# Attention block with a peer mixture: which chunks of the output projection use plain products, and which engine prepares wo's combinations

## The chip, the cores and the metric

The kernel runs on one core of a Trainium2 chip. The metric is device time in microseconds for one launch. Before the change the median of three runs is 1894.39 us (1894.09 to 1894.46).

## The reference

Two branches see the same x (2048 tokens, 1024 features). Branch a is multi-head attention with 32 heads of 32 features, followed by an output projection with wo (1024 x 1024). Branch b picks one expert of 64 per token and head. A gate mixes them.

```python
g = sigmoid((x * gate_w).sum(-1))
qkv = x @ wqkv;  q, k, v = 32 heads of 32
p = softmax(q @ k.T * 32**-0.5)
a = (p @ v).reshape(2048, 1024) @ wo
b = sum over heads of gelu(x . u[e]) * v[e]      # e: the best expert by two small keys
out = g * a + (1 - g) * b
```

## The kernel before

All products run in pairs of rounded numbers: a number is split into a high part (rounded to the type fp32r) and a low part (the rest), and a product of two numbers becomes three matmuls, high by high, high by low, low by high. `split(hi, lo, src)` (L91) does this with a copy on ScalarE (L92) and a subtraction on VectorE (L93).

**Stages.** First queries and keys (L328), then the router of branch b (L404), then the values x @ wv in two halves of 512 columns (L569), then attention by heads (scores L773, exponentials on ScalarE L783, weighted values L794), then the output projection, which the profile calls the tail here.

**Value stage.** `values(ts, half)` makes tiles of 128 tokens, 24 matmuls each; `values_out` (L572) copies each from PSUM to SBUF on ScalarE and stores it by ScalarE's own DMA queue. The last tile goes to a PSUM tile named "o" that belongs to the pool of the next stage, and VectorE copies it out (L575). Between the tiles 4 to 13 of the second half stand `load_early` and `split_early` in turns (L691): they load blocks of wo, form four combinations of them (VectorE, L669), split each (ScalarE copy to a tile "th" of which there are two, VectorE subtraction in place) and store both parts to DRAM tensors t0 to t3, each with h and l for the parts. There are four such rounds of four blocks and a fifth one for the expert table v (tensors vph, vpl). These combinations are those of a Strassen-like scheme.

**Tail.** The 2048 tokens are projected in eight chunks of 256 (`W`). A chunk of the attention output (OC, read from od) is first scaled by one over the row sums times the gate (RB, read from rd).

- Chunk 0 uses plain products: `wo_mm` (L980), 12 matmuls for each of the 8 blocks `kc` of 128 features, 96 in all, on four PSUM banks. Their operands OH and OL, and wo's parts woh and wol, are split as they go (`split_hi`, `split_lo`, L1003 to L1015). The block kc = 7 needs the row sums of the last four heads.
- Chunks 1 to 7 use the scheme with seven products instead of eight: `unit(n)` (L1133) makes 7 `product`s (L1063, 12 matmuls each, L1070) with operands A11, S3, S1, S2, A12, S4, A22 that `operand` (L1048) splits, and with blocks of wo (B11, B21, B22) or the stored combinations (T1 to T4, loaded by `load_t`, L1025). Branch b is added by `av_mm` (L987), 8 matmuls a chunk, so a unit has 92 matmuls and a plain chunk 104.
- While a unit runs, `ahead` prepares the operands of the next chunk. For chunk 1 there is no unit before it: its first product A11 B11 is placed before block kc = 7 of chunk 0, its operands are made between, and the scaling of chunk 2 begins only after the first products of `unit(1)` (L1205).

**The row sums' way.** `finish(H - 1)` and `norm_sums` store the last head's output and sums (od, smd); `load_r` reads the sums of the last group back (rr), `norm_r` takes reciprocals and stores them (rd), and `load_chunk` reads them in a broadcast (rb for chunk 0, the tile accd for others). All of these are DMAs on SyncE's queue (SP), and in order there; only the blocks 0 to 6 of chunk 1 are loaded by GpSimd's queue (L1081). In the same SP queue stand the loads of the combinations: T3 = t2 ahead of the store to smd (L1084), T1 = t0 between the read of rr and the store to rd (L1097), T2 = t1 after (L1104), T4 = t3 after chunk 2 (L1123). Each is 2 MB in its two parts.

**Places.** PSUM has eight banks, named pa0 to pa7 in the tail and used in turn. `post` is the space of rb0, reused for results before their stores. z0, z1 and the two "acc" tiles are reused for operands.

Of the kernel before, what the change touches and what calls it, by code (L numbers as in the profile page):

```python
# [9 lines left out]
F32 = mybir.dt.float32  # L10
F32R = mybir.dt.float32r
# [5 lines left out]
S = 2048  # L17
# [6 lines left out]
W = 256  # L24
# [6 lines left out]
def gated_mha_peer_kernel(ctx, tc, xT, wqkv, wv, wo, wq, k12, ug, v, out):  # L31
# [59 lines left out]
    def split(hi, lo, src, on=None):  # L91
        nc.scalar.activation(hi, src, AF.Copy)  # L92
        (on or nc.vector).tensor_tensor(out=lo, in0=src, in1=hi.bitcast(F32), op=OP.subtract)  # L93
# [8 lines left out]
    def bank():  # L102
        i = bank_no[0] % 8
        bank_no[0] += 1
        return ps1.tile([128, 512], F32, name=f"bk{i}")
# [455 lines left out]
    def values(ts, half, bank=bank):  # L561
        ps = [bank() for _ in ts]
        for kc in range(KC):
            wh, wl = WV[half, kc]
            for t, p in zip(ts, ps):
                tok = slice(t * 128, (t + 1) * 128)
                for a, b, first, last in ((xh, wh, kc == 0, False), (xh, wl, False, False),
                                          (xl, wh, False, kc == KC - 1)):
                    nc.tensor.matmul(p, a[:, kc, tok], b, start=first, stop=last)  # L569
        return ts, ps, half  # L570

    def values_out(ts, ps, half, copy=lambda o, p: nc.scalar.activation(o, p, AF.Copy)):  # L572
        for t, p in zip(ts, ps):
            o = vw.tile([128, 512], F32, name="vo")
            copy(o, p)  # L575
            dma(VD[half][t * 128:(t + 1) * 128, :], o, nc.scalar)
# [70 lines left out]
    load_kq(0, Z)  # L647
    load_shift(0, Z)
    values_out(*fin0)
    values_out(*values(list(range(4)), 1))  # L650

# [11 lines left out]
                    dma(raw[j][64 * k:64 * k + 64, :], v[:, j * 512:(j + 1) * 512])  # L665

    def split_early(i):
        def sub(out, a, b):
            nc.vector.tensor_tensor(out=out, in0=a, in1=b, op=OP.subtract)  # L669

        def parts(t, dst_hi, dst_lo):
            hi, lo = th.tile([128, 512], F32R, name="th"), t.bitcast(F32R)
            split(hi, lo, t)
            dma(dst_hi, hi)
            dma(dst_lo, lo)

        if i < KC // 2:
            b11, b12, b21, b22 = (raw[j] for j in range(4))
            sub(b11, b12, b11)
            sub(b12, b22, b12)  # L680
            sub(b22, b22, b11)
            sub(b21, b21, b22)
            for k, t in enumerate((b11, b22, b12, b21)):
                parts(t, *(d[:, i, :] for d in TD[k]))
        else:
            for j in range(2):
                parts(raw[j], *(d[:, j * 512:(j + 1) * 512] for d in VPD))

    for t in range(4, NT - 1):
        values_out(*values([t], 1))  # L690
        (load_early, split_early)[t % 2](t // 2 - 2) if t < NT - 2 else None  # L691

    ps1.close()
    pso = Pool("pso", space=PSUM, side="right")
# [277 lines left out]
        AT[n] = fin.tile([128, W], F32R, name="at", bufs=3)  # L972
        dma(AT[n], ATD[:, n * W:(n + 1) * W])

    def wo_mm(pa, kcs, first, last):
        for kc in kcs:
            wh, wl = (W0[0][:, 0], W0[0][:, 1]) if kc == 0 else (woh[kc], wol[kc])
            for a, b, i in ((OH[0], wh, 0), (OH[0], wl, 1), (OL[0], wh, 2)):
                for tt, half in pa:
                    nc.tensor.matmul(pa[tt, half], a[:, kc, tt * 128:(tt + 1) * 128],  # L980
                                     b[:, half * 512:(half + 1) * 512],
                                     start=(first and kc == kcs[0] and i == 0),
                                     stop=(last and kc == kcs[-1] and i == 2))
# [36 lines left out]
    def places(t, *names):  # L1020
        t = t.rearrange("p (a k m) -> p a k m", k=HC, m=128)
        for i, name in enumerate(names):
            AP[name] = t[:, 2 * i], t[:, 2 * i + 1]
# [39 lines left out]
    def product(a, b, *av):  # L1063
# [8 lines left out]
                                 stop=(k == HC - 1 and i == 1))  # L1072
        return ps

    ps_odd = None
    pa = {(i, half): bank() for i in range(W // 128) for half in range(2)}
    wo_mm(pa, [0], True, False)
    finish(H - 1)
    sm = pso.tile([128, 512], F32, name="o")
    list(rowsum(sm, *(P[H - 1, NT - i] for i in (1, 2)), ACC.pop(H - 1)))  # L1080
    load_chunk(1, 0, KC - 1, nc.gpsimd)  # L1081
    for n in range(2):
        load_at(n)
    load_t(2, [zp.tile([128, S], F32R, name="z1")], [fin.tile([128, S], F32R, name="t3l")])  # L1084
    places(fin.tile([128, S], F32R, name="s31"), "S3", "S1")
    places(wk.tile([128, S], F32R, name="acc"), "A11", "A12")
    split_hi(1)
    for kc in range(1, KC - 1):
        split_hi(kc + 1)
        if kc == 1:  # L1090
            norm_sums(H - 1, sm)
            load_r(G - 1)
            pso.close()
        split_lo(kc)
        if kc == 4:

            load_t(0, *([keep.tile([128, S], F32R, name=f"wo_raw{i}")] for i in range(2)))  # L1097
        wo_mm(pa, [kc], False, False)
    norm_r(G - 1)
    for n in range(2):  # L1100
        load_chunk(n, KC - 1, KC)
    split_lo(KC - 1)
    split(woh[0], wol[0], raw_wo(0))
    load_t(1, *([keep.tile([128, S], F32R, name=f"wo_raw{i}")] for i in range(2, 4)))  # L1104
    ps_odd = Pool("ps_odd", space=PSUM)
    for (i, half), ps in pa.items():
        av_mm(0, i, half, ps)
    scale_o(1, 0)
    operand(1, "A11")
    BP.update({f"B{i + 1}{j + 1}": [[part[i * HC + k][:, j * 512:(j + 1) * 512] for k in range(HC)]  # L1110
                                    for part in (woh, wol)] for i in range(2) for j in range(2)})
    p1 = product("A11", "B11")
    o = OC[0][:, KC - 1, :]
    nc.vector.tensor_mul(o, o, RB[0][:, KC - 1, :])
    split(OH[0][:, KC - 1, :], OL[0][:, KC - 1, :], o)
    wo_mm(pa, [KC - 1], False, True)
    operand(1, "S3")
    scale_o(1, 1)
    operand(1, "S1")
    load_chunk(2, 0, KC)  # L1120
    load_at(2)

    load_t(3, *([part[k][:, 512:] for k in range(HC)] for part in (woh, wol)))  # L1123
    places(zp.tile([128, S], F32R, name="z0"), "S2")
    places(wk.tile([128, S], F32R, name="acc"), "S4", "A22")
    post = rb0.rearrange("p k m -> p (k m)").rearrange("p (a m) -> p a m", m=512)

    def osb():
        return wk.tile([128, 512], F32, name="osb")

    ORDER = ("A11", "S3", "S1", "S2", "A12", "S4", "A22")

    def unit(n, p1):  # L1133


        u2, u3, u5 = (post[:, i] for i in range(3))
        last = n == S // W - 1

        def ahead(*names):
            if last:  # L1140
                return
            for name in names:
                if name == "A11":
                    scale_o(n + 1, 0)
                    scale_o(n + 1, 1)
                operand(n + 1, name)

        c1 = osb()
        nc.scalar.activation(c1, p1, AF.Copy)
        if n == 1:  # L1150
            for (i, half), ps in pa.items():
                r = osb() if i == half == 0 else post[:, 2 * i + half]
                if half:
                    nc.scalar.activation(r, ps, AF.Copy)
                else:
                    nc.vector.tensor_copy(r, ps)
                store(0, i, half, r)
            for name in ("S2", "A12", "S4", "A22"):
                operand(n, name)
        if n + 2 < S // W:  # L1160
            load_chunk(n + 2, 0, KC)
            load_at(n + 2)
        if n > 1:
            ahead("A11")
        p7 = product("S3", "T3")
        if n > 1:
            ahead("S3")
        p5 = product("S1", "T1")
        if n > 1:
            ahead("S1")  # L1170
        p6 = product("S2", "T2")
        tt(u2, c1, p6)
        tt(u3, u2, p7)
        tt(u2, u2, p5)
        tt(u5, u3, p5)
        if n > 1:
            ahead("S2")

        def c11():
            p2 = product("A12", "B21", n, 0, 0)  # L1180
            pieces = 2 if last else 1
            for i in range(pieces):
                c = slice(i * 512 // pieces, (i + 1) * 512 // pieces)
                tt(c1[:, c], c1[:, c], p2[:, c])
                store(n, 0, 0, c1, c)

        def c12():
            p3 = product("S4", "B22", n, 0, 1)
            tt(u2, u2, p3)
            store(n, 0, 1, u2)  # L1190

        def c22():
            ps = bank()
            av_mm(n, 1, 1, ps, True, True)
            tt(u5, u5, ps)
            store(n, 1, 1, u5)

        def c21():
            p4 = product("A22", "T4", n, 1, 0)
            tt(u3, u3, p4)  # L1200
            store(n, 1, 0, u3)

        if not last:
            c11()
            ahead(*((() if n > 1 else ORDER[:4]) + ("A12",)))  # L1205
        c12()
        ahead("S4")
        c22()
        c21()
        ahead("A22")  # L1210
        if last:
            c11()

    for n in range(1, S // W):
        unit(n, p1 if n == 1 else product("A11", "B11"))
    ps_odd.close()
    ps_even.close()
    fin.close()
# [32 lines left out]
```

## Time and profile before

| what | value |
|---|---|
| median of 3 runs | 1894.39 us |
| the profiled execution, its own time | 1892.16 us |
| span of its trace | 1890.4 us |
| mean granted TensorE clock | 0.995 |
| TensorE busy | 1860.9 us (98% of the span), 10187 matmuls |
| VectorE busy | 1285.2 us (68%) |
| ScalarE busy | 1179.9 us (62%) |
| GpSimd busy | 148.8 us (8%) |

The 1.8 us between the span and the execution's time lie before and after the traced instructions. A group of the profile is named out<-in by the program's tile names; "idle before, releaser" says how long the engine stood still ahead of the instruction and what ended this. "PEclk" or "granted clock" is the share of full speed at which the throttle let TensorE run. Where matmuls follow one another without a wait, their starts are 0.227 us apart in this kernel (128x128 by 512 columns), although each one's own duration is about 0.39 us, since they are pipelined.

The stages on the trace's clock: queries and keys to 391 us, router to 481 us, values 481 to 668 us, attention 668 to 1696 us, the tail from there to the end.

### The profile page before, as it was taken

How to read it: one execution, taken by the hardware profiler on the slowest of the kernel's cores; microseconds unless marked ns; L12 is line 12 of the kernel's file. 1: busy time of each engine (PE TensorE's matmuls, PEld its weight loads, DVE VectorE, ACT ScalarE, POOL GpSimd, SP SyncE). 2: the span in 40 equal slices, each digit the busy share in tenths (PEclk: the TensorE clock that was granted, in tenths of full speed). 3: DMA queues.
4: the chain of work that ended last, by engine and by line, in shares of the span. 5: the costliest groups of instructions: out<-in, count | busy, mean ns of one | idle time of the engine just before them, and what ended most of it. 6: DMA issues, size and time to landing. Idle time of an engine off the chain costs nothing.

```text
span 1890.4 us, 25992 instructions
## 1 busy us (share of the span) xinstructions
PE 1860.9 (98%) x10187; PEld 1143.2 (60%) x10187; DVE 1285.2 (68%) x1066; ACT 1179.9 (62%) x1461; POOL 148.8 (8%) x183
## 2 busy tenths in 40 slices
PE   9999999999999899999999999999999999998899
PEld 7877777888888654444444444444444444446787
DVE  4522224867521368888888888888888888885774
ACT  4211111200222289999999999999999999992221
POOL 0000000035200000000000000000000000010000
PEclk9999999999999999999999999999999999999999
DMA  5777774420234767777778787777777777757651
GB/s 211 279 269 258 263 271 138 137 73 2 79 103 145 257 163 169 158 176 157 178 161 191 161 186 163 182 167 179 175 168 174 160 166 176 184 123 251 211 172 57
DMA packets 118468, 325.81 MB, mean 172 GB/s; under 512 B 15892, under 2 KB 50084, under 8 KB 94088
## 3 DMA queue, kind: packets, MB, share of 16 engines
q1 hardware_dynamic: 80904, 177.83, 30.8%
q0 software_dynamic: 14976, 103.29, 26.3%
q10 hardware_dynamic: 22464, 43.00, 7.1%
q8 instruction: 81, 1.33, 0.3%
q14 instruction: 43, 0.35, 0.1%
HBM read 152.36 MB, written 72.10 MB: 119 GB/s over the span
## 4 chain that ended last, share of the span: by engine, by line
PE 93%; DMA 4%; DVE 1%; ACT 1%; SPq 0%; issue 0%; ACTq 0%; DVEq 0%
PE ring L773 28%; PE o L794 25%; PE bk L328 16%; PE pa L1070 7%; PE bk L569 6%; PE bk L404 5%; PE bk L214 2%; PE bk L275 2%; PE ring L807 1%; DMA smd<-ssb 1%; DMA t1h<-th 1%; PE pa L987 1%; DMA t3l<-wvraw 1%; DMA wvraw<-in_wo 1%; PE pa L980 0%; SPq L74 0%
## 5 line engine op out<-in xcount | busy, mean ns | idle before, releaser
L783 ACT ACTIVATE P<-ring 128x512 f32<-128x512 f32 (+2 forms) x1034 | 914.8, 983 | 21.8 <-PE ring L773 8.3
L822 DVE TENSOR_TENSOR acc<-acc,P 128x2048 f32<-128x2048 f32 x319 | 731.0, 2292 | 74.6 <-ACT P L783 48.5
L794 PE MATMUL o<-P,V 128*32 128x512 f32 x3840 | 464.8, 599 | 0.0
L773 PE MATMUL ring<-z,z 98*128 98x512 f32 x1024 | 272.2, 407 | 1.4 <-ACT P L783 1.1
L773 PE MATMUL ring<-Q,K 98*128 98x512 f32 x1024 | 271.7, 407 | 0.2 <-ACT P L783 0.2
L773 PEld LDWEIGHTS ring<-z,z 98*128 98x128 f32 x1024 | 182.0, 188 | 144.8 <-ACT P L783 76.0
L773 PEld LDWEIGHTS ring<-Q,K 98*128 98x128 f32 x1024 | 182.1, 188 | 143.8 <-ACT P L783 73.8
L794 PEld LDWEIGHTS o<-P,V 128*32 128x32 f32 x3840 | 98.8, 109 | 223.1 <-issue 214.2
L92 ACT ACTIVATE hi<-bk 128x512 fp32r<-128x512 f32 x64 | 37.6, 598 | 242.7 <-PE bk L328 226.6
L328 PE MATMUL bk<-xh,whi 128*128 128x512 f32 x448 | 176.2, 393 | 0.1
L328 PE MATMUL bk<-xh,wlo 128*128 128x512 f32 x448 | 174.4, 389 | 0.0
L328 PE MATMUL bk<-xl,whi 128*128 128x512 f32 x448 | 174.4, 389 | 0.0
L93 DVE TENSOR_TENSOR lo<-bk,hi 128x512 fp32r<-128x512 f32 x64 | 44.1, 690 | 188.5 <-ACT hi L92 184.1
L816 POOL DMA_DIRECT2D accd<-P x95 | 81.6, 859 | 1108.0 <-ACT P L783 622.8
L820 DVE TENSOR_TENSOR acc<-P 128x2048 f32<-128x2048 f32 x32 | 73.4, 2292 | 74.2 <-ACT P L783 74.2
L328 PEld LDWEIGHTS bk<-xh,whi 128*128 128x128 f32 x448 | 84.1, 188 | 24.2 <-issue 6.7
L569 PE MATMUL bk<-wvh,xh 128*128 128x512 f32 x248 | 96.7, 390 | 0.0
L569 PE MATMUL bk<-wvh,xl 128*128 128x512 f32 x248 | 96.5, 389 | 0.0
L569 PE MATMUL bk<-wvl,xh 128*128 128x512 f32 x248 | 96.5, 389 | 0.0
L328 PEld LDWEIGHTS bk<-xh,wlo 128*128 128x128 f32 x448 | 84.1, 188 | 17.7
L328 PEld LDWEIGHTS bk<-xl,whi 128*128 128x128 f32 x448 | 84.2, 188 | 17.0
L1070 PE MATMUL pa<-woh,acc 128*128 128x512 f32 x224 | 74.4, 397 | 7.8 <-ACT acc L92 7.8
(189 smaller groups left out, 1703.8 us busy)
## 6 DMA issues: line engine op xcount, KB each, us to landing
accd<-P POOLq DMA_DIRECT2D x95, 1024.0 KB, 7.5
wqt<-in_wq SPq DMA_DIRECT2D x32, 1024.0 KB
vd<-vo ACTq DMA_DIRECT2D x32, 256.0 KB
z<-kdh SPq DMA_DIRECT2D x32, 256.0 KB
z<-qdh SPq DMA_DIRECT2D x32, 256.0 KB
V<-vd SPq DMA_DIRECT2D x32, 256.0 KB
K<-kdh SPq DMA_DIRECT2D x32, 256.0 KB
Q<-qdh SPq DMA_DIRECT2D x32, 256.0 KB
```

The lines of the kernel that those rows point to most:

```text
L93: (on or nc.vector).tensor_tensor(out=lo, in0=src, in1=hi.bitcast(F32), op=OP.subtract)
L214: nc.tensor.matmul(b0[w, n], w0[w][a][:, kc, :], b[:, kc, n * 512:(n + 1) * 512], start=(kc == 0 and i == 0), stop=(kc == KC - 1 and i == 2))
L328: nc.tensor.matmul(ps, a[:, kc, :], b[:, kc, n * 512:(n + 1) * 512], start=first, stop=last)
L404: nc.tensor.matmul(ps, a[:, kc, tok], b, start=first, stop=last)
L569: nc.tensor.matmul(p, a[:, kc, tok], b, start=first, stop=last)
L773: on_ring(nc.tensor.matmul(ring[:, i, :], K[:98, kt * 128:(kt + 1) * 128], Q[:98, qc * 512:(qc + 1) * 512], start=True, stop=True), i)
L783: on_ring(nc.scalar.activation(P[h, kt][:, q0 * 512:(q0 + m) * 512].rearrange("p (a m) -> p a m", a=m), ring[:, i:i + m, :], AF.Exp, scale ...
L794: nc.tensor.matmul(O[h][32 * qc:32 * qc + 32, :], Vt[g][:, kt, 32 * j:32 * j + 32], p[:, qc * 512:(qc + 1) * 512], start=(kt == 0), stop=( ...
L816: nc.gpsimd.dma_start(ACCD[h], P[h, kt], accum_op=OP.add)
L820: nc.vector.tensor_add(ACC[h], P[h, 0], P[h, kt])
L822: nc.vector.tensor_add(ACC[h], ACC[h], P[h, kt])
L1070: nc.tensor.matmul(ps, AP[a][i][:, k, :], BP[b][j][k], start=(not av and k == 0 and i == j == 0), stop=(k == HC - 1 and i == 1))
```

## The change

In the value stage the four rounds and the fifth stand in one piece ahead of the second half's first tile, and VectorE alone does the splits: `tensor_copy` in place of ScalarE's copy. In the tail chunk 1 is made by plain products as chunk 0 is, on the other four banks; the scheme begins with chunk 2. The store to smd, the read of rr and the store to rd no longer have loads of combinations ahead of them: T1, T2 and T3 are loaded after the last blocks of the chunks 0 and 1. GpSimd's queue is as it was.

```diff
     values_out(*fin0)
-    values_out(*values(list(range(4)), 1))
...
         def parts(t, dst_hi, dst_lo):
             hi, lo = th.tile([128, 512], F32R, name="th"), t.bitcast(F32R)
-            split(hi, lo, t)
+            nc.vector.tensor_copy(hi, t)
+            sub(lo, t, hi.bitcast(F32))
...
+    for i in range(KC // 2 + 1):
+        load_early(i)
+        split_early(i)
+    values_out(*values(list(range(4)), 1))
     for t in range(4, NT - 1):
         values_out(*values([t], 1))
-        (load_early, split_early)[t % 2](t // 2 - 2) if t < NT - 2 else None
...
-    def wo_mm(pa, kcs, first, last):
+    def wo_mm(pa, n, kcs, first, last):
...
+    def plain_out(n, pa):
+        for i, ((j, half), ps) in enumerate(pa.items()):
+            if i % 2:
+                nc.scalar.activation(post[:, i], ps, AF.Copy)
+            else:
+                nc.vector.tensor_copy(post[:, i], ps)
+            store(n, j, half, post[:, i])
+
+    def split_o(n, k0, k1):
+        o = OC[n][:, k0:k1, :]
+        nc.vector.tensor_mul(o, o, RB[n][:, k0:k1, :])
+        split(OH[n][:, k0:k1, :], OL[n][:, k0:k1, :], o)
...
-    load_t(2, [zp.tile([128, S], F32R, name="z1")], [fin.tile([128, S], F32R, name="t3l")])
...
-        if kc == 4:
-
-            load_t(0, *([keep.tile([128, S], F32R, name=f"wo_raw{i}")] for i in range(2)))
-        wo_mm(pa, [kc], False, False)
+        wo_mm(pa, 0, [kc], False, False)
     norm_r(G - 1)
     for n in range(2):
         load_chunk(n, KC - 1, KC)
     split_lo(KC - 1)
     split(woh[0], wol[0], raw_wo(0))
-    load_t(1, *([keep.tile([128, S], F32R, name=f"wo_raw{i}")] for i in range(2, 4)))
+    for i in range(2):
+        load_t(i, *([keep.tile([128, S], F32R, name=f"wo_raw{2 * i + j}")] for j in range(2)))
     ps_odd = Pool("ps_odd", space=PSUM)
     for (i, half), ps in pa.items():
         av_mm(0, i, half, ps)
-    scale_o(1, 0)
-    operand(1, "A11")
-    p1 = product("A11", "B11")
...
+    split_o(0, KC - 1, KC)
+    wo_mm(pa, 0, [KC - 1], False, True)
+    OH[1] = zp.tile([128, KC, W], F32R, name="z1")
+    OL[1] = wk.tile([128, KC, W], F32R, name="acc")
+    for k0, k1 in ((0, HC), (HC, KC)):
+        split_o(1, k0, k1)
+    load_chunk(2, 0, KC)
+    load_at(2)
+    load_t(2, [zp.tile([128, S], F32R, name="z0")], [fin.tile([128, S], F32R, name="t3l")])
+    pa1 = banks4()
+    wo_mm(pa1, 1, list(range(KC - 1)), True, False)
+    for (i, half), ps in pa1.items():
+        av_mm(1, i, half, ps)
+    plain_out(0, pa)
+    load_chunk(3, 0, KC)
+    places(wk.tile([128, S], F32R, name="acc"), "A11", "A12")
+    places(fin.tile([128, S], F32R, name="s31"), "S3", "S1")
+    for i in range(2):
+        scale_o(2, i)
+    for name in ("A11", "S3", "S1", "A12"):
+        operand(2, name)
+    wo_mm(pa1, 1, [KC - 1], False, True)
+    places(zp.tile([128, S], F32R, name="z1"), "S2")
+    places(wk.tile([128, S], F32R, name="acc"), "S4", "A22")
+    load_at(3)
+    load_t(3, *([part[k][:, 512:] for k in range(HC)] for part in (woh, wol)))
...
-    def unit(n, p1):
+    def unit(n):
...
+        if n == 2:
+            plain_out(1, pa1)
+            for name in ("S2", "S4", "A22"):
+                operand(n, name)
...
-    for n in range(1, S // W):
-        unit(n, p1 if n == 1 else product("A11", "B11"))
+    for n in range(2, S // W):
+        unit(n)
```

More of the change, by code (lines that the diff above doesn't have):

```diff
@@ L973, in load_at @@
         dma(AT[n], ATD[:, n * W:(n + 1) * W])
-    def wo_mm(pa, kcs, first, last):
+    def wo_mm(pa, n, kcs, first, last):
         for kc in kcs:
-            wh, wl = (W0[0][:, 0], W0[0][:, 1]) if kc == 0 else (woh[kc], wol[kc])
-            for a, b, i in ((OH[0], wh, 0), (OH[0], wl, 1), (OL[0], wh, 2)):
+            wh, wl = (W0[0][:, 0], W0[0][:, 1]) if n == kc == 0 else (woh[kc], wol[kc])
+            for a, b, i in ((OH[n], wh, 0), (OH[n], wl, 1), (OL[n], wh, 2)):
                 for tt, half in pa:
@@ L1073, in product, with banks4 @@
         return ps
+    post = rb0.rearrange("p k m -> p (k m)").rearrange("p (a m) -> p a m", m=512)
+    def plain_out(n, pa):
[9 more added lines that the diff above has]
+        split(OH[n][:, k0:k1, :], OL[n][:, k0:k1, :], o)
+    def banks4():
+        return {(i, half): bank() for i in range(W // 128) for half in range(2)}
     ps_odd = None
-    pa = {(i, half): bank() for i in range(W // 128) for half in range(2)}
-    wo_mm(pa, [0], True, False)
+    pa = banks4()
+    wo_mm(pa, 0, [0], True, False)
     finish(H - 1)
@@ L1083, in gated_mha_peer_kernel @@
         load_at(n)
-    load_t(2, [zp.tile([128, S], F32R, name="z1")], [fin.tile([128, S], F32R, name="t3l")])
-    places(fin.tile([128, S], F32R, name="s31"), "S3", "S1")
-    places(wk.tile([128, S], F32R, name="acc"), "A11", "A12")
     split_hi(1)
@@ L1107, in gated_mha_peer_kernel @@
         av_mm(0, i, half, ps)
-    scale_o(1, 0)
-    operand(1, "A11")
+    split_o(0, KC - 1, KC)
[24 more added lines that the diff above has]
+    load_t(3, *([part[k][:, 512:] for k in range(HC)] for part in (woh, wol)))
     BP.update({f"B{i + 1}{j + 1}": [[part[i * HC + k][:, j * 512:(j + 1) * 512] for k in range(HC)]
                                     for part in (woh, wol)] for i in range(2) for j in range(2)})
-    p1 = product("A11", "B11")
[L1113 to L1126, printed above, removed]
     def osb():
         return wk.tile([128, 512], F32, name="osb")
-    ORDER = ("A11", "S3", "S1", "S2", "A12", "S4", "A22")
-    def unit(n, p1):
+    def unit(n):
         u2, u3, u5 = (post[:, i] for i in range(3))
@@ L1146, in ahead @@
                 operand(n + 1, name)
+        p1 = product("A11", "B11")
         c1 = osb()
         nc.scalar.activation(c1, p1, AF.Copy)
[L1150 to L1158, printed above, removed]
+        if n == 2:
+            plain_out(1, pa1)
+            for name in ("S2", "S4", "A22"):
                 operand(n, name)
@@ L1162, in unit @@
             load_at(n + 2)
-        if n > 1:
-            ahead("A11")
+        ahead("A11")
         p7 = product("S3", "T3")
-        if n > 1:
-            ahead("S3")
+        ahead("S3")
         p5 = product("S1", "T1")
-        if n > 1:
-            ahead("S1")
+        ahead("S1")
         p6 = product("S2", "T2")
@@ L1175, in unit @@
         tt(u5, u3, p5)
-        if n > 1:
-            ahead("S2")
+        ahead("S2")
         def c11():
@@ L1204, in unit @@
             c11()
-            ahead(*((() if n > 1 else ORDER[:4]) + ("A12",)))
+            ahead("A12")
         c12()
```

## The prediction

> **What bounds the kernel now.** The page's first part says TensorE, busy 98% of the span. So only the remaining holes, and the time in which it ran at half clock, can be won. I read the waits of TensorE over the value stage first, then the timelines of TensorE and ScalarE there.
>
> ```profile
> PE o L569 <- ACT vo L572: 9.1, 1, 9.1
> ```
> ```profile
> 658.49 0.63 ACT L92 ACTIVATE th<-wvraw 128x512 fp32r<-128x512 f32 x1 [4.05 <-DMA wvraw<-in_v]
> ...
> 659.96 0.58 ACT L572 ACTIVATE vo<-bk 128x512 f32<-128x512 f32 x1
> ```
> ```profile
> 660.59 0.80 PE L569 MATMUL o<-wvh,xh 128*128 128x512 f32 x1 [9.06 <-ACT vo L572]
> ```
>
> One hole of 9.06 us: the last tile of the values waits for the copy of the tile before it. That tile's matmuls end at 651.53, yet its copy runs at 659.96, because ScalarE, in order, stands before the th copies of the combinations, which wait for DMAs.
>
> Next the tail's timeline of TensorE (every line with a hole), its windows, and the chain of waits.
>
> ```profile
> 1723.21 0.50 PE L1070 MATMUL pa<-woh,acc 128*128 128x512 f32 x1 [2.73 <-ACT acc L92]
> ...
> 1729.11 2.07 PE L980 MATMUL pa<-woh,z 128*128 128x512 f32 x4 [2.61 <-ACT z L92]
> ...
> 1751.35 0.50 PE L1070 MATMUL pa<-wol,acc 128*128 128x512 f32 x1 [0.66 <-DMA wol<-t3l]
> ...
> 1759.29 0.80 PE L1070 MATMUL pa<-woh,acc 128*128 128x512 f32 x1 [5.12 <-ACT acc L92]
> ```
> ```profile
> 1730.00:1735.00 5.00, 5.00 (x13) 3.84 (x13) 3.58 (x6) 2.23 (x5) 0.00 (x0) 0.50 0.92 367
> 1735.00:1740.00 5.00, 5.00 (x23) 4.08 (x22) 3.54 (x7) 2.41 (x6) 0.00 (x0) 0.97 0.88 285
> ```
> ```profile
> 1702.80 13.81 DMA smd<-ssb
> ...
> 1716.63 1.63 DMA rr<-smd
> ...
> 1719.12 5.49 DMA rd<-rr
> ...
> 1725.97 1.99 DMA rb<-rd
> ...
> 1729.11 5.49 PE pa L980 x12
> ```
>
> See four holes, 11.1 us together, and in the windows (granted clock, DMA share, GB/s last) a clock of 0.50 after the first two. The chain shows why chunk 0's block 7 is late: an 8 KB store, smd, takes 13.81 us to land, where the read of rr takes 1.63. Ahead of it in SP's queue stand the two 1 MB loads of T3 (issued 1699.42 and 1700.72); ahead of rd, which takes 5.49, stand T1's. The last hole is A11 of chunk 2: ahead of it in VectorE's order stands a sum into `post`, which waits 10.9 us for the stores out<-rb, and these had 2 MB of T4 before them.
>
> **Value stage.** VectorE takes the th copies, so ScalarE has only the tile copies. From the rows: matmul end 651.53, 0.04 to the copy, 0.63 from its start to the next matmul (659.96 to 660.59): the last tile starts at 652.20 instead of 660.59, **8.4 us** won. Its 24 matmuls lasted 6.93 (660.59 to 667.52), partly at half clock; at 0.227 each they last 5.4, with 0.1 for the short hole: **1.4 us** more.
>
> What hides the moved work: a round of combinations took about 14.8 us (starts 605.41, 621.13, 635.13, 649.80). A th copy on VectorE isn't in the trace; bounds are 0.35 (half the 1024-element TENSOR_SCALAR of 0.69) and 0.69 (a 512-element subtraction). I take 0.69, the nearest in size: a round grows to at most 15.8. Its first blocks are there at 580.3, so four rounds end at 643.5 and the fifth at about 648.5, from its rows (loads to stores 7 us). Queued behind it are VectorE's copy of the last tile and SP's loads of V, both due at 657.7: 9 us of cover. If a round took over 18, each further microsecond would count four times.
>
> **Tail.** From the end of branch b's matmuls for chunk 0 (last start slot 1720.31) to the last matmul's end, 1886.38, are 166.07 us with 12 + 7 x 92 = 656 matmuls, 148.8 us at 0.2268. So holes and slow clock hold 17.3. After: 12 for block 7, 104 for chunk 1, 6 x 92 = 668, 151.5 us. Added work is 12 matmuls, **2.7 us**; won at most 17.3, net **14.6**, if no hole is left. Three things decide that.
>
> *Row sums.* From smd's landing to TensorE's start were 12.5 us (1716.61 to 1729.11), 3.5 of them rd's excess over the 1.99 of rb. Without T1 and T3 ahead that is 9.0, and block 7 is due at 1720.31: smd must land by 1711.3. The price of smd alone is not in the trace. Lower end: 1.63, as rr, hence 1704.4. Upper end: GpSimd's 1.8 MB for chunk 1 (q0) holds it up; of the 4.5 MB moved from 1696 to 1718, T3's 2.1 MB go, and the rest at the 298 GB/s of 1700 to 1712 ends near 1709, so it lands at 1711. I take 1706, nearest rr. VectorE reaches the reciprocals at 1710.8 anyway (end of L1014), so block 7's operands come at 1718.5: no hole, 1.8 us to spare. Wait added: behind block 7 stands chunk 1, but that needs the same chain only through VectorE's order: its first high parts follow 2.7 us later, just the time of block 7.
>
> [...] The row: after holes of 2.73 and 2.61 the clock was 0.50 and 12 matmuls lasted 5.48 instead of 2.72. [...]
>
> *Loads for chunk 2.* SP issues T1 from about 1717.9 on, then T2, chunk 2, T3, the stores of chunk 0, chunk 3, T4: 4.2, 2.2, 2.1, 1.05, 2.2, 2.1 MB. Rates by the rows, at full DMA share: 400 GB/s for whole loads (367 at 0.92), 300 for chunks (a steady unit: 196 at 0.64), 330 for stores and T4 (1745 to 1750). With 1.6 to start, landings are: T2 1730, chunk 2 1737.4, T3 1742.6, stores 1746, chunk 3 1753, T4 1760. Due: plain products keep TensorE busy until 1720.31 + 116 x 0.2268 = 1746.6. A11 needs chunk 2 and 3.8 us (two scalings of 1.18, ScalarE 0.63, VectorE 0.69, handoffs): ready 1741.2 of 1746.6. T3 due 1749.3. S2 follows the stores by 4: 1750 of 1754.8. T4 due 1764.7. Everything has 4 to 7 us: the plain chunk is the cover, and in place of one hole it gives room for the next.
>
> *VectorE* in the first unit has the steady 17.7 us plus `plain_out` 1.4 and the three operands with handoffs 4.2, over 20.85, but starts with A11 to A12 done; the next A11 is due at 1767.5 and ready near 1759. No cost.
>
> **Sum.** 8.4 + 1.4 + 14.6 = 24.4 us. The profiled execution took 1892.16 (span 1890.4 and 1.8 around it): 1867.8 after, span 1866. The median of the runs lies 2.2 above that execution; I forecast on the median, **1870 us**. A difference under 0.2%, 3.8 us, can't be told from none.
>
> **Rivals.**
> - *The sums stay late.* Against: the 1.63 of rr. For: the landing of smd without T3 isn't in the trace, GpSimd's queue stays. If nothing changes, block 7 starts at 1729.11, a hole of 8.8 and 2.8 of slow clock: 1870 + 12 = **1882**.
> - *Loads at 250 GB/s* (between the 300 taken and the 198 of SP's queue from 1700 to 1712, shared with GpSimd's). A11 2.4 late, T3 1.9 more, S2 3.7, T4 2.4, slow clock 3: **1883**.
> - *The combinations aren't hidden*, or the last tile waits all the same: the 9.8 are lost, **1880**.
> - *Slower: one convoy.* All the loads now lie between 1718 and 1760, in one order. At 200 GB/s T2 lands at 1740.5, chunk 2 at 1751.7, T3 at 1762, T4 at 1789: holes of 8.9, 3.9, 4.9, 6.8 and 5 of slow clock, 29 in all: **1899**. It decides from below about 210 GB/s. For it: the 198 above. Against: that queue had a rival then, GpSimd's last transfers landing before 1718.
>
> **Chances.** Forecast 0.68 (1867 to 1875), sums late 0.10, 250 GB/s 0.08, not hidden 0.04, convoy 0.10, of which a part ends near no change. Faster by over 0.2% 0.90, within it 0.03, slower 0.07. The range runs from 1867 (no short hole, and a run as low as the profiled one against its median) to 1880, which takes in half of the first two rivals; above it lie about 2 in 10.
>
> **What the profile after would show.** Right: TensorE's hole ahead of the last value tile under 1 us; smd landing before 1711; block 7 on the heels of branch b; no window at 0.50 in the tail; A11 of chunk 2 ready before TensorE asks. Wrong: a hole at block 7 released by ScalarE's z (sums), at the first A11 (chunk 2), at T3 or T4 released by a DMA (convoy), or ahead of the first scores (combinations).

## The result and the profile after

The changed kernel takes 1874.66 us (median of four runs, 1872.07 to 1875.96), the kernel before 1894.43 beside it (1894.09 to 1895.19). The ratio is 0.9893 with a 95% interval of 0.9876 to 0.9911: 19.8 us faster, where 24.4 were forecast. The profiled execution took 1872.07 us (span 1870.3, mean granted clock 0.999), 20.1 less than the profiled one of before, so the two traces can be set against each other stage by stage.

| step | forecast, us | by the two traces, us |
|---|---|---|
| last value tile starts earlier | 8.4 | 8.4 (660.59 to 652.59, and the values had begun 0.4 later) |
| its 24 matmuls at full clock | 1.4 | 1.4 (6.93 to 5.57) |
| begin of the values, behind the matmuls of L619 | 0 | -0.4 (542.71 to 543.09) |
| attention, first score to first matmul of the tail | 0 | **-2.0** (1028.86 to 1030.83) |
| tail, from there to the span's end | 14.6 | **12.7** (194.02 to 181.31) |
| sum | 24.4 | 20.1 |

**Value stage.** The waits of TensorE from 540 to 690 us (in total, times, longest), then ScalarE's timeline:

```profile
PE o L569 <- ACT vo L572: 0.7, 1, 0.7
```
```profile
641.06 0.60 ACT L572 ACTIVATE vo<-bk 128x512 f32<-128x512 f32 x1 [4.84 <-PE bk L569]
...
651.94 0.60 ACT L572 ACTIVATE vo<-bk 128x512 f32<-128x512 f32 x1 [4.84 <-PE bk L569]
```

ScalarE copies a tile out every 5.44 us (one copy between these two is left out), each time as soon as TensorE is done: no copy stands behind a th copy any more. What is left of the 9.06 us is one handoff of 0.69.

**The attention's start**, which no step of the forecast touched. TensorE's timeline, then the windows (granted clock, DMA share and GB/s last):

```profile
660.30 0.49 PE L777 MATMUL ring<-z,z 98*128 98x512 f32 x1 [0.36 <-ACT P L787]
661.64 0.96 PE L777 MATMUL ring<-z,z 98*128 98x512 f32 x3 [0.85 <-ACT P L787]
662.98 2.10 PE L777 MATMUL ring<-z,z 98*128 98x512 f32 x5 [0.38 <-ACT accd L787]
```
```profile
660.00:665.00 5.00, 3.47 (x9) 1.82 (x9) 1.36 (x1) 5.00 (x6) 0.00 (x0) 0.85 1.09 316
665.00:670.00 5.00, 5.00 (x29) 2.17 (x32) 2.29 (x1) 3.67 (x5) 0.93 (x1) 0.81 1.02 227
```

Three holes, none of them over 0.85, and the clock falls to 0.85 and 0.81 in the two windows: five scores take 2.10 us. In the trace of before the same groups stand with 0.23, 0.84 and 0.38, and the five scores take 1.48 at a clock of 1.00.

**Tail.** TensorE has two short holes left of the four. Its timeline:

```profile
1712.92 1.15 PE L984 MATMUL pa<-woh,z 128*128 128x512 f32 x4
...
1739.61 0.40 PE L1074 MATMUL pa<-wol,acc 128*128 128x512 f32 x1
1740.33 0.74 PE L1074 MATMUL pa<-woh,acc 128*128 128x512 f32 x2 [0.33 <-DVE acc L93]
...
1759.23 0.50 PE L1074 MATMUL pa<-wol,acc 128*128 128x512 f32 x1 [0.66 <-DMA wol<-t3l]
```

Block 7 (1712.92) follows branch b's last matmul without a hole, though its operand z is there only at 1712.82. The low part of A11 of chunk 2 and the low part of T4 come a little late. The chain of waits, the windows and VectorE's timeline show why:

```profile
1695.40 7.84 DMA smd<-ssb
...
1714.08 11.28 DMA wo_raw<-t1l
...
1727.22 9.96 DMA accd<-rd
```
```profile
1725.00:1730.00 5.00, 5.00 (x24) 4.14 (x23) 0.00 (x0) 0.00 (x0) 0.00 (x0) 1.00 0.84 252
1730.00:1735.00 5.00, 5.00 (x24) 4.14 (x23) 0.00 (x0) 0.00 (x0) 0.00 (x0) 1.00 0.57 167
```
```profile
1737.31 2.36 DVE L1050 TENSOR_TENSOR V<-V,accd 128x1024 f32<-128x1024 f32 x2 [15.85 <-DMA accd<-rd]
```

The store of the row sums still takes 7.84 us, without a load of the combinations ahead of it on its queue. And the last of the four broadcast loads of chunk 2's scales (accd<-rd, 256 KB each) lands 9.96 us after its issue: VectorE has stood still for 15.85 us by then. In the windows it is these loads that move little at a middling DMA share. The view of the DMA queues says what they are made of:

```profile
DMA packets 741, 4.07 MB, mean 407 GB/s; under 512 B 78, under 2 KB 268, under 8 KB 268
```
```profile
DMA packets 1469, 2.09 MB, mean 209 GB/s; under 512 B 108, under 2 KB 1372, under 8 KB 1372
```

The first line is the stretch 1715 to 1725 us, T1 and T2 with the first of chunk 2's own rows; the second 1727 to 1737, in which chunk 2's scales land. Nearly all packets of the second are under 2 KB, and half as many bytes move. The small packets alone are not the reason, as two shorter stretches show: 1725 to 1727.5, in which most of chunk 2's rows land (V<-od, ahead of the scales on the queue), and 1728 to 1733.5, the scales.

```profile
DMA packets 966, 0.88 MB, mean 350 GB/s; under 512 B 111, under 2 KB 966, under 8 KB 966
DMA packets 720, 0.70 MB, mean 127 GB/s; under 512 B 38, under 2 KB 720, under 8 KB 720
```

All packets of both are under 2 KB, and the rows move 350 GB/s, the scales 127. A load of scales reads each row for 32 partitions and writes these 32 alone; which of the two slows it, no run here separates.

### The profile page after: what moved, and what is told of

It is laid out like the page before. It is cut to its first block, busy times and chain, and to the rows that moved or that the text cites. A ratio compares the mean times of both kernels' runs of the same rounds, so it can differ in the third digit from the quotient of the medians.

```text
span 1870.3 us, 25976 instructions
## 1 busy us (share of the span) xinstructions
PE 1859.0 (99%) x10199; PEld 1141.8 (61%) x10199; DVE 1284.0 (69%) x1069; ACT 1168.1 (62%) x1439; POOL 148.8 (8%) x183
## 4 chain that ended last, share of the span: by engine, by line
PE 94%; DMA 4%; ACT 1%; DVE 0%; issue 0%; SPq 0%; DVEq 0%; ACTq 0%
PE ring L777 28%; PE o L798 25%; PE bk L328 16%; PE bk L569 9%; PE pa L1074 6%; PE bk L404 5%; PE bk L275 2%; PE ring L811 1%; PE bk L214 1%; DMA w0raw<-in_wqkv 1%; DMA accd<-P 1%; DMA wo_raw<-t1l 1%; DMA accd<-rd 1%; PE pa L991 0%; DMA smd<-ssb 0%; DMA wol<-t3l 0%
## 5 line engine op out<-in xcount | busy, mean ns | idle before, releaser
L572 ACT ACTIVATE vo<-bk 128x512 f32<-128x512 f32 x31 | 18.5, 598 | 108.7 <-PE bk L569 97.9
```

## The experiments

The theory after this profile: the two parts of the change are independent and add up; the value part wins because no tile copy stands behind a combination on ScalarE any more; the tail part wins because the plain chunk gives cover while the loads that stood ahead of the row sums come later; what is missing of the forecast is half clock at the attention's start and broadcast loads slower than assumed. Rivals: one part hides the other's loss; the place of the combinations counts and not the engine; the row sums are early because the loads moved, and the plain chunk only costs.

Every time below is a median. Two holes or lengths are set beside each other by the kernels' profiles; attention and tail are cut as in the table above.

### E1 and E2: each part alone

E1 is the kernel before with the value stage of the change; E2 is the changed kernel with the old value stage.

```diff
 E2, against the changed kernel
-            nc.vector.tensor_copy(hi, t)
-            sub(lo, t, hi.bitcast(F32))
+            split(hi, lo, t)
...
-    for i in range(KC // 2 + 1):
-        load_early(i)
-        split_early(i)
...
+        (load_early, split_early)[t % 2](t // 2 - 2) if t < NT - 2 else None
```

> The kernel before with the value stage's part alone: combinations ahead of the tiles, split by VectorE alone; the tail as before. Theory (two separate gains that add up): the hole ahead of the last value tile goes from 9.06 to 0.7 us and its matmuls run at full clock, 9.4 us less than before in all (1885), less up to 1.5 us if the start of the attention falls to half clock as it did in the changed kernel. Rival (the gains hang together, the tail profits from earlier combinations): well under 9 us.

> The changed kernel with the value stage as it was before (ScalarE splits, between the tiles). Theory: the 9.06 us hole is back, the tail from the first projection matmul to the last is 177.3 us as in the changed kernel instead of 190.0; the time is 12 to 13 us under before (1882). Rival: under 11 or over 15.

E1: 1885.40 us (ratio to the kernel before 0.9951, 0.9935 to 0.9968), against 1894.32 beside it 8.9 won. E2: 1883.04 (0.9933, 0.9913 to 0.9952), 11.3 won. Together 20.2, and the whole change brought 19.8: the parts add up within the spread of the runs, which is wide for E2 (1880.23 to 1887.91), and neither hides much of the other. E2 won a little less than the 12 to 13 expected. TensorE's waits over the value stage in E1, then in E2:

```profile
PE o L569 <- ACT vo L572: 0.7, 1, 0.7
```
```profile
PE o L569 <- ACT vo L572: 10.0, 1, 10.0
```

E1 also has the tail of before, its 8.0 us of holes at A11 and 3.1 at block 7, and smd in 13.75 us.

### E3: VectorE alone, in the old places

```diff
-    for i in range(KC // 2 + 1):
-        load_early(i)
-        split_early(i)
...
+        (load_early, split_early)[t % 2](t // 2 - 2) if t < NT - 2 else None
```

> The changed kernel, VectorE alone splits, but the rounds stand between the value tiles as before. Theory (it is the engine that counts, since VectorE and SP have nothing else in that stage, so their order among themselves is the same): same time as the changed kernel, 1874.7 within 1.5 us, hole ahead of the last tile 0.7. Rival (the place ahead is what counts): the hole stays at several us, 1880 or more.

1873.43 us (0.9889, 0.9872 to 0.9905), 1.2 below the changed kernel, whose runs spread over 3.9: no difference. Ahead of the last value tile its trace shows 0.69 us as well. It is the engine that counts; with VectorE, that the combinations stand in one piece ahead of the tiles adds nothing. ScalarE's copies in the place ahead of the tiles were not run.

### E5: the loads moved, but no plain chunk

Chunk 1 by the scheme as before, T1 to T3 loaded after the row sums.

```diff
-    wo_mm(pa1, 1, list(range(KC - 1)), True, False)
...
+    p1 = product("A11", "B11")
...
-    for n in range(2, S // W):
-        unit(n)
+    for n in range(1, S // W):
+        unit(n, p1 if n == 1 else product("A11", "B11"))
```

> The changed value stage, and in the tail chunk 1 by the scheme again (12 matmuls less), but with the loads of T3, T1, T2 behind the last blocks of chunks 0 and 1, as in the changed kernel. Theory (the plain chunk is the cover under which the loads land): block 7 of chunk 0 starts without a hole, but S3 waits for T3 by about 1, S1 for T1 by 3, S2 for T2 by 2, A22 for T4 by up to 9, A11 of chunk 2 by 5, with 3 to 5 of slow clock and 2.7 less work: 10 to 20 us over the changed kernel (1885 to 1895). Rival (the order of the queue is the whole gain): 2.7 us under the changed kernel, 1872.

1887.61 us (0.9963, 0.9949 to 0.9977): 13 above the changed kernel. TensorE's waits in its tail:

```profile
PE pa L1073 <- ACT acc L92: 3.4, 1, 3.4
PE pa L1073 <- DMA woh<-t3h: 2.8, 1, 2.8
PE pa L1073 <- DMA wol<-t3l: 2.0, 1, 2.0
PE pa L1073 <- DMA wo_raw<-t1l: 1.9, 1, 1.9
PE pa L1073 <- DMA t3l<-t2l: 1.9, 1, 1.9
...
```

Block 7 has no hole, but now each of the four combinations comes late in its turn (T1, left out above, by 0.5), and A11 too, 12.5 us in all. So moving the loads alone trades the old waits for others, and is 2.2 us slower than E1, which has the same value stage and the tail of before; the 12 matmuls that a plain chunk costs more (2.7 us) buy the time in which the loads land.

### E6 and E7: what holds up the row sums

E6 puts 2 MB in front of smd on SP's queue again (one part of T3, loaded twice); E7 takes the 1.8 MB of chunk 1 from GpSimd's queue and loads them on SP's, after the row sums.

```diff
 E6
+    early = [fin.tile([128, S], F32R, name=name) for name in ("t3l", "s31")]
+    for t in early:
+        dma(t, TD[2][1].rearrange("p k m -> p (k m)"))
...
 E7
-    load_chunk(1, 0, KC - 1, nc.gpsimd)
...
-    for n in range(2):
-        load_chunk(n, KC - 1, KC)
+    load_chunk(0, KC - 1, KC)
+    load_chunk(1, 0, KC)
```

> The changed kernel with two loads of 1 MB (the low part of T3, once to its place and once to the place of S3 and S1, which is overwritten later) in SP's queue ahead of the store smd, where before had T3. Theory (the queue's order is what made the sums late): smd takes 13 to 14 us to land instead of 7.8, block 7 of chunk 0 starts with a hole of 5 to 6 us and 2 to 3 of slow clock, 7 to 9 us over the changed kernel. Rival (GpSimd's 1.8 MB set smd's landing, the rest is hidden): within 1.5 us of the changed kernel.

> The changed kernel with blocks 0 to 6 of chunk 1 loaded by SP behind block 7 of chunk 0 instead of by GpSimd's queue ahead of everything. Measures smd's landing with nothing beside it. Theory (the 7.8 us come from GpSimd's transfers): 2 to 3.5 us, and block 7 is ready some 4 us before TensorE asks; in exchange chunk 1 lands near 1720 and its first matmul waits 5 to 9 us, so the time is 5 to 12 us over the changed kernel. Rival (a store to DRAM behind the head's other stores takes that long by itself): over 6 us.

The chain of waits of E6, and SP's timeline of E7, where the read of rr is issued when smd has landed:

```profile
1693.67 13.71 DMA smd<-ssb
1707.39 1.65 DMA rr<-smd
```
```profile
1693.49 0.50 SPq L74 DMA_DIRECT2D smd<-ssb  x1
1695.19 0.31 SPq L74 DMA_DIRECT2D rr<-smd  x1
```

So the same 8 KB take **1.70 us** with neither, **7.84** beside GpSimd's 1.8 MB (7.3 to 8.0 in every kernel here that has these loads alone beside it), and **13.71** with 2 MB ahead on SP's queue besides. Both causes are real, some 6 us each. In the changed kernel's queue view for 1695 to 1704, GpSimd's queue holds 67.2% of the engines' time. How the DMA engines divide their time between the queues, no run here shows.

By time, E6 takes 1876.9 us (0.9901, 0.9885 to 0.9917), 2.2 above the changed kernel and not the 7 to 9 expected. Its hole at block 7 is the expected one:

```profile
1715.77 2.08 PE L984 MATMUL pa<-woh,z 128*128 128x512 f32 x4 [4.42 <-ACT z L92]
```

with 1.6 of half clock behind it (its 12 matmuls hold 4.3 us instead of 2.7). But no hole comes after it, since all later loads have had that time to land: 6.0 lost at block 7, the 1.6 of the changed kernel's late loads given back, and the tail is 4.5 longer (185.85). The rest of the difference between 4.5 and 2.2 lies in the attention, which runs at full clock in this profile (1029.73), and in the spread of the runs. So with the plain chunk in place, 2 MB ahead of the row sums cost little: most of the tail's gain is the plain chunk's cover, less of it the order of the queue. A kernel with the plain chunk and both T1 and T3 at their old places was not run.

E7 takes 1881.03 us (0.9922, 0.9902 to 0.9942): the row sums come early, and chunk 1's scales, now behind them, late, a hole of 9.62 at chunk 1's first matmul.

### E9: the loads in the order in which they are needed

Chunk 2 ahead of T1 and T2, T4 ahead of chunk 3.

```diff
-    for i in range(2):
-        load_t(i, *([keep.tile([128, S], F32R, name=f"wo_raw{2 * i + j}")] for j in range(2)))
     ps_odd = Pool("ps_odd", space=PSUM)
...
     load_chunk(2, 0, KC)
     load_at(2)
+    for i in range(2):
+        load_t(i, *([keep.tile([128, S], F32R, name=f"wo_raw{2 * i + j}")] for j in range(2)))
     load_t(2, [zp.tile([128, S], F32R, name="z0")], [fin.tile([128, S], F32R, name="t3l")])
...
+    load_t(3, *([part[k][:, 512:] for k in range(HC)] for part in (woh, wol)))
     load_chunk(3, 0, KC)
...
-    load_t(3, *([part[k][:, 512:] for k in range(HC)] for part in (woh, wol)))
```

> The changed kernel with SP's loads in the order of need: chunk 2 ahead of T1 and T2, T4 ahead of chunk 3. Theory (chunk loads took 10 us, far slower than the forecast's 300 GB/s, and used up the cover): the holes of 0.33 at A11 of chunk 2 and 0.66 at T4 go, 1 to 1.5 us under the changed kernel. Rival: T1 or T2, now later, make a hole of their own and nothing is won.

1879.79 us (0.9915, 0.99 to 0.9929), 5.1 **above** the changed kernel: the theory fell. TensorE's waits in its tail:

```profile
PE pa L1074 <- DVE rb L1043: 3.0, 1, 3.0
PE pa L1074 <- DMA t3l<-t2l: 1.9, 1, 1.9
PE pa L1074 <- ACT acc L92: 1.1, 1, 1.1
...
```

The scales of chunk 2 took 8.76 us though neither T1 nor T2 was ahead of them, so A11 is late all the same (1.1, and 0.3 for its low part), and now T3 lands 17.89 us after its issue; with it the stores of chunk 0 are late, for which a copy on VectorE waits 9.42 us ahead of S3 (3.0). So these broadcast loads are slow without T1 and T2 ahead of them too (8.76 us for 9.96), and put first they delay the large ones: T3's low part is 1.9 late here and not late in the changed kernel.

### E10: the last store of the value stage on another queue

In the changed kernel the second of two stores on ScalarE's queue is issued at 659.14, 0.5 us ahead of the first exponential. E10 gives this store to GpSimd's queue.

```diff
-    def values_out(ts, ps, half, copy=lambda o, p: nc.scalar.activation(o, p, AF.Copy)):
+    def values_out(ts, ps, half, copy=lambda o, p: nc.scalar.activation(o, p, AF.Copy), queue=nc.scalar):
...
-            dma(VD[half][t * 128:(t + 1) * 128, :], o, nc.scalar)
+            dma(VD[half][t * 128:(t + 1) * 128, :], o, queue)
...
-               nc.vector.tensor_copy)
+               nc.vector.tensor_copy, nc.gpsimd)
```

> The changed kernel with the last value tile's store issued from GpSimd's queue, so that ScalarE doesn't stand 1.0 us behind VectorE's copy of that tile before the first exponential. Theory (the holes of 0.36, 0.85 and 0.38 at the start of the attention are why the clock falls to half there, which cost 1.5 us against before): the holes shrink by 1 us in sum, the first 21 matmuls after them run at full clock, 1 to 2.5 us under the changed kernel. Rival (the half clock comes from where a window happens to fall): 0 to 1 us.

1871.18 us (0.9872, 0.9856 to 0.9888), 3.5 below the changed kernel by the medians, more than expected. It is 2.0 below the same kernel's second set of runs (E13), and the intervals of the ratios overlap, so the size of the gain is uncertain. TensorE's timeline at the attention's start:

```profile
660.63 0.96 PE L777 MATMUL ring<-z,z 98*128 98x512 f32 x3 [0.63 <-ACT P L787]
661.97 1.48 PE L777 MATMUL ring<-z,z 98*128 98x512 f32 x5 [0.38 <-ACT accd L787]
```

One hole of the three is gone, 0.6 us, and the five scores take 1.48: full clock. The attention lasts 1028.08 us, 2.75 less than in the changed kernel's first profile; the tail is 1.1 longer (182.4), and the two profiled runs are 1.8 apart.

### E12 and E13: what is left, and how much of it changes from run to run

E12 is E10 with chunk 0's block 7 behind four blocks of chunk 1, so that the row sums have 10.9 us more, and T1 at its old place. E13 is the changed kernel once more.

```diff
 E12, against E10
+        if kc == 4:
+            load_t(0, *([keep.tile([128, S], F32R, name=f"wo_raw{j}")] for j in range(2)))
...
-    wo_mm(pa1, 1, list(range(KC - 1)), True, False)
+    wo_mm(pa1, 1, list(range(HC)), True, False)
+    wo_mm(pa, 0, [KC - 1], False, True)
+    wo_mm(pa1, 1, list(range(HC, KC - 1)), False, False)
```

> The kernel e10 (last store of the value stage by GpSimd's queue) with the tail in another order: chunk 0's block 7 stands behind the blocks 0 to 3 of chunk 1, 48 matmuls (10.9 us) later, VectorE prepares the first half of chunk 1 while the row sums travel, and T1 is loaded at its old place between the read of rr and the store to rd, some 10 us earlier. Theory (what is left in the tail is that the loads of chunk 2 and T4 land a little late, since all loads start only after the row sums): chunk 2 and T4 land 4 to 5 us earlier, the tail's holes (0.45 at block 7, 0.34 at the first A11, 0.62 at T4 in e10's profile) go, no other comes, and the time is 1.4 to 2 us below e10's 1871.2: 1869 to 1870. Rival (the broadcast loads are limited by themselves or by other transfers, not by their start): the hole at A11 stays or grows, time within 1 us of e10's. Second rival (the row sums come over 11 us later, or chunk 1's operands are not ready at 1712.5): a hole of 1 to 4 us at chunk 1's first matmul or at block 7, 1873 or more.

> The changed kernel once more, on the same chip as e12. Theory (the 4 us between runs of one and the same kernel, 1872.1 to 1876.0, are TensorE's clock in the first 10 us of the attention after the three short holes, where five profiles show 0.62 to 0.85 and four show 1.00): the runs' times go with the mean granted clock, about 2 us for each 0.001 of it (0.001 of 1870 is 1.87), and the holes in the profile are the same as in the first profile of this kernel (0.69, 0.36, 0.85, 0.38, 0.33, 0.66, each within 0.15). Rival (the spread is late landings): holes of another length in the profile, or times that spread by over 3 us at one and the same mean clock.

E12: 1869.76 us (0.9862, 0.9845 to 0.9879). The number is the theory's, the trace is not. TensorE's waits in its tail:

```profile
PE pa L1074 <- DMA wol<-t3l: 1.4, 1, 1.4
PE pa L1074 <- DMA t3l<-t2l: 0.6, 1, 0.6
```

The holes at block 7 and A11 are gone, but T4's low part is 1.4 late and T3's 0.6: 2.0 us of holes for E10's 1.6, and the tail is no shorter (182.3 for 182.4). T4 lands 71.1 us after the tail's first matmul, in E10 71.2: its chain goes over chunk 2's scales (8.82) and the stores of chunk 0 (11.29), and T1's earlier start does not shorten those. That is the first rival's reason. The 1.4 us between the medians are not shown to be more than the spread of E10's runs (1870.3 to 1872.4). E12 and E10 are both below the changed kernel by the medians, and are not told apart.

E13: 1873.22 us (0.9883, 0.9865 to 0.9902), with runs of 1870.26, 1872.83, 1873.61 and 1875.55 at mean clocks of 0.999, 0.999, 0.998 and 0.998. So time and clock go together as the theory had it, as far as three digits of the mean clock can show. But the profiled run (1870.26) has the three holes at the attention's start with clocks of 0.85 and 0.81, as the first profile of this kernel had, and lacks the hole at A11 and half of the one at T4 (0.34). These 0.65 us of holes and a value stage that began earlier (last tile at 651.83 for 652.59) make up 1.4 of the 1.8 us between the two profiled runs; with the low clock this run is as fast as E10's profiled one (1870.29). The spread has both causes: clock and landings.

That the same holes may or may not cost the clock is seen across kernels. With 0.23 or 0.36 us, then 0.84 or 0.85, then up to 0.38, the windows 660 to 665 and 665 to 670 show 0.85 and 0.81 in the changed kernel (twice) and E9, 0.69 and 0.63 in E3, 0.62 and 0.70 in E5, but 1.00 in E1, E6 and E7; in before, where the same groups stand 9 us later, it is 1.00 as well, and in E2, where they stand 12 us later, it is 0.50 from 675 to 680. So the length of the holes alone does not tell the outcome: 0.36, 0.85 and 0.38 go with clocks of 0.85 and 0.81 in E9, and with 1.00 in E7. In the changed kernel the three holes lie between 659.9 and 663.0, and TensorE has matmuls in between.

The clock records of the traces show more. From the values to the last matmul, before has half clock for 6.83, 6.83 and 3.41 us (from 656.73, 1728.51 and 1759.23), the changed kernel for 3.41 (from 663.51), and before's changes lie whole multiples of 3.41 us apart: 312 from 663.55 to 1728.51, 7 from 1735.34 to 1759.23. Where the windows of an experiment hold a whole stretch, they add up to 3.4, 6.8 or 10.2 us of half clock (10.2 in E7, from 1719.0 on). Cut along such a grid of 3.41 us, TensorE stands idle for 1.13 (E9) to 1.43 us (the changed kernel, 660.09 to 663.51) in one cell at the attention's start in each of the six profiles with the low clock, and the clock falls at the end of that cell. In the four others with the same holes the grid divides them, and the larger share is 0.86 (E7), 0.87 (before), 1.02 (E6) and 1.16 us (E1). So in these ten profiles the outcome goes with where the grid falls. E10 and E12 have only 1.01 us of holes there, less than any cell that cost the clock there. The ten show no sharp limit in idle time (1.13 did, 1.16 did not; the matmuls' ends are modelled), and the tail shows other numbers: a cell with 1.86 us passed at full clock in E5, and 1.52 (1721.68 to 1725.10) in before, while one with 1.87 did not in E9.

## Why the forecast came out as it did

**Right.** The direction, and 19.8 of 24.4 us.

- *Value stage:* 9.7 of the 9.8 forecast. The th copy on VectorE, taken at 0.69 with 0.35 as the lower bound, takes 0.42; this did not matter, since the fifth round's last part is stored from 648.0 on (648.5 was forecast), and V is loaded from 658.4 on. E3 narrows the reason: with VectorE as the engine the place does not matter.
- *Block 7 has no hole:* right, but the step *"I take 1706, nearest rr"* was wrong in size. On before's clock (the tail starts 7.4 earlier now) smd lands at 1710.6, against the 1711.3 at which it must: it met the upper bound, whose reason was GpSimd's load, and E7 shows that reason to be the cause (1.70 us without that load, 7.84 with it). Choosing the nearest row took an undisturbed transfer as a measure for a disturbed one. The 1.8 us to spare were not there: z came 0.1 us ahead of the matmul that needed it, so that no hole came was in part luck.
- *A plain chunk costs 2.7 and serves as cover:* right (E5: without it, 13 lost; E6: with it, 2 MB ahead of the row sums cost 2.2).
- Of the signs named for the profile after, four came true (hole ahead of the last value tile 0.69; smd before 1711; block 7 without a hole; full clock in the tail, 1.00 up to the last matmul), one did not: A11 of chunk 2 was late.

**Wrong, 4.3 us of 24.4.**

- *"Everything has 4 to 7 us"* failed in two terms. The smaller is the start: T1 was issued at 1720.0 on before's clock and not at 1717.9, since the row sums came later than taken. The larger is *"300 for chunks"*. T1 and T2 moved as forecast: 4.2 MB in 12.7 us from first issue to landing, 12.1 expected. From T2's landing to chunk 2's are 11.8 us for 2.2 MB, 185 GB/s, where 7.4 were forecast; the scales alone, 1.05 MB in 9.96, are 105. Chunk 2 lands at 1744.6 on before's clock (1737.4 forecast: 2.1 by the start, 0.6 by T1 and T2, 4.4 by its own loads), T4 at 1766.6 (1760). The forecast had scaled a steady unit's 196 GB/s at a DMA share of 0.64 up to a full share, as if the idle share could be filled; the stretch 1728 to 1733.5 at a share of 0.55 with 127 GB/s shows that it is not filled while these loads run. E9 confirms it: first in the queue they took 8.76. The cover of 5.4 us at A11 was used up, and 0.68 us were lost there and 0.95 at T4 (12 matmuls each, by their starts). With 0.10 at block 7 that is 1.7 of the 1.9 us that the tail fell short; 0.2 stay without a place.
- *The attention had no term.* The forecast took it as unchanged. Its three holes stood in the trace of before, but at full clock. 2.0 us were lost there, 1.5 of them in 5 scores and 16 value matmuls (4.80 us from the start of the one to the next scores, 662.98 to 667.78; 3.27 in before, 672.21 to 675.48) and 0.1 in the first hole; 0.3 stay without a place. E10, which takes away one of these holes, wins 2.75 in the attention of its profile. The clock is 1.1 to 1.6 of it, since E1, E6 and E7 have the same holes at full clock and an attention of 1029.2 to 1029.7 us; 0.6 are the hole. Whether the clock falls goes, in these profiles, with how the grid of 3.41 us cuts the holes (E13).

**The rivals.** *Sums late* did not come, by 0.7 us; its price of 12 was too high, for E6 makes smd that late (13.71, though rd behind it takes only 1.44) and is 2.2 above the changed kernel. *250 GB/s* named the right wait, A11 first; its price of 13 us did not come, because only the broadcast loads were that slow (105) and the whole ones ran at 407. The same kept the *convoy* away. *Not hidden* did not come.

## What to carry to other kernels

When loads are moved out of a chain's way, ask what they were under cover of before: moved alone they won nothing (E5), and the plain chunk was worth its extra matmuls only as time in which they land. Price a transfer by a row of its own kind and with its own neighbours on the other queues: 8 KB took 1.70, 7.84 or 13.71 us, and the broadcast loads moved 105 GB/s, a quarter of the 407 of the whole ones. After a hole has been closed, read the short holes that follow it too: what passed at full clock before may not do so any more, and moving one store there was worth 2.0 or 3.5 us by the two sets of runs.

## What was not expected of the hardware

- Loads of scales to 32 partitions at a time, 4 x 256 KB in packets under 2 KB, move 105 GB/s (9.96 us) at a DMA share of 0.55 (1728 to 1733.5); rows in packets as small moved 350 on the same queue, and T1 and T2 in 1 MB loads 407.
- An 8 KB store is held up about 6 us by 1.8 MB on another engine's queue (1.70 to 7.84), as much as by 2 MB ahead on its own (7.84 to 13.71).
- Three holes of at most 0.36, 0.85 and 0.38 us within 3.5 us cost part of the clock in six of ten profiles with the same code at that place, and the stretches at half clock are 3.41 us long in the changed kernel and 3.41 or 6.83 in before, on one grid of 3.41 us.
